# Moving operands of the first layer laid out as two runs, narrow blocks that alternate two feature chunks, and a new order

## The chip, the cores and the metric

One core of a Trainium2 chip runs the whole program. The time is the device time of one execution in microseconds (us); lower is better.

## What is computed

Attention with a block-causal mask, its heads laid side by side to 2304 tokens of 512 features, then two feed-forward layers.

```python
scores = scale * q @ k.T            # 4 batches, 8 heads, 576 tokens, 64 features a head
attn = softmax(where(block_i >= block_j, scores, -1e9))      # blocks of 64 tokens
x = (attn @ v) -> (2304, 512)
h = x @ w_in                        # 512 -> 2048
g = where(h >= 1, h, where(h <= -1, 0, (h + 1) ** 2 / 4))
x = g @ w_out                       # 2048 -> 512
h = x @ w2_in;  g = maximum(0.01 * h, h);  out = g @ w2_out  # second layer, the same sizes
```

## The kernel before, in words

Every product of the two layers is made of three matmuls in a 32-bit type that TensorE rounds (fp32r): both factors are split into a rounded part (hi) and the rest (lo), and hi*hi, hi*lo and lo*hi are summed in PSUM. A matmul holds one operand of 128x128 in the array (the stationary one, loaded anew for each matmul) and streams the other (the moving one) past it, column by column.

**Stage 1, attention with the first layer's h.** Attention is done in units of a head pair (lines L651 scores, L743 transposes, L762 and L770 values; scores and values use a quarter or a half of the array at a time). Between these, x @ w_in is done by blocks of tokens (`BLOCKS`): three narrow blocks of 256 tokens in `h1_block` (L877 for the first two pairs of feature chunks of block 0, L887 for all others) and three wide ones of 512 tokens in `h1_wide` (L855). The weights are stationary, x is the moving operand. In a narrow block two feature chunks j of 128 share one PSUM bank, 256 columns each; all 12 matmuls of chunk 0 run, then those of chunk 1, in pieces of four (kc = 0 to 3). A wide chunk fills a bank with 512 columns. `xbuf` gives x its places, `moe_load` fetches blocks 1 to 5 from DRAM (L813) and splits them (L815 on ScalarE, L816 on VectorE); block 0 is split where attention leaves it (`unit_values`). `w_float` makes the weights' halves (L508 to L523).

**Stage 2, the first layer's sums.** g @ w_out is done by a scheme with seven products in place of eight on half-size blocks (`ORDER`, `PRODUCTS`). The first 384 positions go through `y_group` (L1191), the other 768 through `y_unit` with `wide` true, three units of 256 positions. A unit takes eight steps p; each step loads four blocks of g, forms four differences (`t_forms`, L1211), splits both into hi and lo (L1236, L1237 on ScalarE, L1238, L1240 on VectorE), and does 7 products x 3 parts x 2 halves t = 42 matmuls of 256 columns (L1252). The weights are stationary; the moving operand, 256 positions of g, is one contiguous run, and serves both t.

**Stage 3, the second layer's h** (`h_step`, L1068, 288 columns), and **stage 4, the second layer's sums**: `y_unit` with `wide` false, the same 42 matmuls a step, but g is stationary and 256 columns of the weights move. `wc` hands these out as two runs of 128 columns that lie 384 or 512 elements apart:

```python
w = WC[m, p][c][g].get()[:, :, 128 * (i - 3 * g):128 * (i - 3 * g) + 128]
return w if e - a == 256 else w[:, a // 128]
```

Four units have 256 positions (t = 0, 1 take turns on each moving operand, each with its own half of the bank); the last has 128, so that each moving operand is used once and consecutive matmuls of a product add to the same 256 columns of PSUM.

**The order** of all instructions on all engines is made ahead by `Plan`: each step is an op with an engine, a modelled cost and a priority; `schedule` tries 400 list schedules from a random seed (`SEED`) and keeps the best. PE's ops are the groups that one `f` issues. All DMAs go through SP's queue.

Of the kernel before, what the change touches and what calls it, by code (L numbers as in the profile page):

```python
# [14 lines left out]
ALU = mybir.AluOpType  # L15
# [51 lines left out]

ENTRY = 105
SLACKS = (0, 800)
SEED, TRIES = 6, 400  # L70
LATEST, DRAWS = 0, 1


# [299 lines left out]
def fused_kernel(ctx, tc, qk, v, w1, w2, out):  # L373
# [92 lines left out]
    def xbuf(n, size):  # L466

        homes = (A0, A1)[n % 2], *LO[2 * (n % 2):2 * (n % 2) + 2]
        for home in homes:
            home.begin(F32R)  # L470
        hi, lo0, lo1 = (home.reg(0, m * size, shape=lambda ap, m=m: ap.rearrange("p (k t) -> p k t", k=m)) for home, m in zip(homes, (4, 2, 2)))
        return hi, (lo0, lo1)

    def xpart(x, c, kc):

        return (x[1][kc // 2], (kc % 2, kc % 2 + 1)) if c else (x[0], (kc, kc + 1))

    def xview(x, c, kc):
        buf, (k, _) = xpart(x, c, kc)
# [245 lines left out]
    def unit_values(pair, part, prio, ring, evac):  # L725
# [52 lines left out]
        if late is not None:  # L778
            dve(nq, prio, lambda: nc.vector.tensor_tensor(xp.get()[:, 0:nq], s.get()[:, 0, 0:nq], xp.get()[:, 0:nq], op=ALU.mult), [s, xp], [xp])
            if q0:  # L780
                x = XB[0]
                act(q0, prio, lambda: nc.scalar.activation(x[0].get()[:, kc], xp.get()[:, 0:q0], AF.Copy), [xp], [(x[0], (kc, kc + 1))], sb=True)
                dve(q0, prio, lambda: nc.vector.tensor_tensor(
                    xview(x, 1, kc), xp.get()[:, 0:q0], bc(x[0].get()[:, kc]), op=ALU.subtract), [xp, (x[0], (kc, kc + 1))],
                    [xpart(x, 1, kc)], port=True)
            dma(128 * (nq - q0) * 4, prio, lambda: nc.sync.dma_start(x1d[:, kc, c0 + q0:c0 + nq], xp.get()[:, q0:nq]), [xp],
                [(f"x1d{kc}", (c0 + q0, c0 + nq))])
            return
        if q0:
            x = XB[0]  # L790
            act(q0, prio, lambda: nc.scalar.activation(x[0].get()[:, kc], s.get()[:, 0, 0:q0], AF.Copy), [s], [(x[0], (kc, kc + 1))])
            dve(q0, prio, lambda: nc.vector.tensor_tensor(
                xview(x, 1, kc), s.get()[:, 0, 0:q0], bc(x[0].get()[:, kc]), op=ALU.subtract), [s, (x[0], (kc, kc + 1))], [xpart(x, 1, kc)])
        act(nq - q0, prio, lambda: nc.scalar.activation(xp.get()[:, 0:nq - q0], s.get()[:, 0, q0:nq], AF.Copy), [s], [xp])
        dma(128 * (nq - q0) * 4, prio, lambda: nc.sync.dma_start(x1d[:, kc, c0 + q0:c0 + nq], xp.get()[:, 0:nq - q0]), [xp],
            [(f"x1d{kc}", (c0 + q0, c0 + nq))])


    def moe_load(n, prio):
        i, m = BLOCKS[n]  # L800
        x = XB[n] = xbuf(n, 256 * m)
        if i == 0:
            return
        t0, tb = 256 * i, 256 * m
        for k in range(NKC):
            have = [q for _, q, wr in plan.regions.get(f"x1d{k}", []) if wr]
            assert all(any(q[0] <= z < q[1] for q in have) for z in range(t0, t0 + tb, 64)), (i, k)
        for j, lo in enumerate(x[1]):
            hi = (x[0], (2 * j, 2 * j + 2))

            def hv(j=j):
                return x[0].get()[:, 2 * j:2 * j + 2]
            dma(256 * tb * 4, prio, lambda lo=lo, j=j: nc.sync.dma_start(bc(lo.get()), x1d[:, 2 * j:2 * j + 2, t0:t0 + tb]),  # L813
                [(f"x1d{k}", (t0, t0 + tb)) for k in (2 * j, 2 * j + 1)], [lo])
            act(2 * tb, prio + X_SPLIT, lambda hv=hv, lo=lo: nc.scalar.activation(hv(), bc(lo.get()), AF.Copy), [lo], [hi], sb=True)  # L815
            dve(2 * tb, prio + X_SPLIT, lambda hv=hv, lo=lo: nc.vector.tensor_tensor(lo.get(), bc(lo.get()), bc(hv()), op=ALU.subtract),  # L816
                [lo, hi], [lo], port=True)

    def runs(pos0, n):
# [45 lines left out]
    def h1_block(n, p0, dp, hbanks):  # L865

        i, xt = BLOCKS[n][0], XB[n]
        for p in range(NP2):
            pr = p0 + 2 * dp * p
            ps = bank(hbanks[0])  # L870
            hbanks.append(hbanks.pop(0))
            early = i == 0 and p < EARLY
            for kc in range(NKC if early else 0):
                for j in range(2):
                    def f(fc=2 * p + j, j=j, kc=kc, ps=ps):
                        for k, (c, x) in enumerate(((0, 0), (1, 0), (0, 1))):
# [25 lines left out]
            h1_out(ps, parts, pr - 8)  # L902
# [294 lines left out]
    def t_forms(n, pv, raw, tt):  # L1197

        def g(i, k=1):
            return bc(raw.get()[:, n * i:n * (i + k)])  # L1200

        def t(i, k=1):
            return tt.get()[:, n * i:n * (i + k)]

        def two(ap):
            return ap.rearrange("p (s t) -> p s t", s=2)
        for cols, o, r, w, f in (
                (2 * n, 0, [raw], (0, 2), lambda: (two(t(0, 2)), g(3).unsqueeze(1).to_broadcast([128, 2, n]), two(g(1, 2)))),
                (n, 2, [raw, (tt, (0, 1))], (2, 3), lambda: (t(2), g(2), t(0))),
                (n, 3, [raw, (tt, (2, 3))], (3, 4), lambda: (t(3), g(0), t(2)))):  # L1210
            dve(cols, pv, lambda f=f: nc.vector.tensor_tensor(*f(), op=ALU.subtract), r, [(tt, w)], port=True)  # L1211
# [1 line left out]
    def y_unit(layer, pos0, n, p0, dp, banks_):  # L1213
# [11 lines left out]
        for p in range(NP2):  # L1225
# [3 lines left out]
            def s_(t, i, k=1):  # L1229
# [5 lines left out]
            t_forms(n, pv, raw, tt)  # L1235
            act(3 * n, pv, lambda raw=raw, hr=hr: nc.scalar.activation(s_(hr, 0, 3), bc(s_(raw, 0, 3)), AF.Copy), [(raw, (0, 3))], [hr], sb=True)  # L1236
            act(4 * n, pv, lambda tt=tt, ht=ht: nc.scalar.activation(s_(ht, 0, 4), s_(tt, 0, 4), AF.Copy), [tt], [ht], sb=True)  # L1237
            dve(3 * n, pv, lambda raw=raw, hr=hr: nc.vector.tensor_tensor(s_(raw, 0, 3), bc(s_(raw, 0, 3)), bc(s_(hr, 0, 3)), op=ALU.subtract),  # L1238
                [(raw, (0, 3)), hr], [(raw, (0, 3))], port=True)
            dve(4 * n, pv, lambda tt=tt, ht=ht, lt=lt: nc.vector.tensor_tensor(s_(lt, 0, 4), s_(tt, 0, 4), bc(s_(ht, 0, 4)), op=ALU.subtract),  # L1240
                [tt, ht], [lt], port=True)
            for o, m in enumerate(ORDER):
# [1 line left out]
                ps = P[m][0]  # L1244
                wh, zi = WHERE[ri]
                for k, (cw, x) in enumerate(((0, (hr, ht)[wh]), (1, (hr, ht)[wh]), (0, ((raw, (0, 3)), (lt, None))[wh]))):
                    def f(k=k, cw=cw, x=x[0] if isinstance(x, tuple) else x, ps=ps, li=li, zi=zi, p=p):
# [175 lines left out]
```

## Time and profile before

| | |
|---|---|
| three timed runs | 928.88, 934.44, 935.6 us (median 934.44) |
| the profiled execution | 928.28 us, of which the span of its instructions is 926.5 us |
| TensorE (PE) matmul busy | 915.6 us, 99% of the span |
| VectorE (DVE) / ScalarE (ACT) / GpSimd (POOL) busy | 727.7 / 519.6 / 293.9 us |

A matmul's record spans its passage through the array and overlaps with the next, so PE's busy share tells whether it was ever empty, not how fast it went. The pace is read from the chain of work that ended last: a piece such as "452.67 90.69 PE bank L1252 x770" is 770 matmuls that followed each other for 90.69 us.

### The profile page before, as it was taken

The page shows a single profiled execution, that of the slowest core. Times are in us where ns is not written, and L with a number is a line of the kernel's source. Part 1 is how long each engine was busy: PE and PEld are TensorE (multiplying, and loading weights), DVE is VectorE, ACT ScalarE, POOL GpSimd, SP SyncE. Part 2 cuts the span into 40 slices and gives each one's busy share as a digit, 9 for nine tenths or more (in the row PEclk, how much of TensorE's full clock was granted, in tenths as well). Part 3 has the DMA queues.
Part 4 walks back from the last instruction along what each step waited for, and adds up shares of the span by engine and source line. Part 5 has one row for each costly group of instructions (what it writes and reads, how often), then busy time and mean ns, then how long its engine had stood idle before and what let it go on. Part 6 is the DMA issues. An engine that isn't in the chain of part 4 may idle for free.

```text
span 926.5 us, 18684 instructions
## 1 busy us (share of the span) xinstructions
PE 915.6 (99%) x6818; PEld 827.7 (89%) x6818; DVE 727.7 (79%) x1247; ACT 519.6 (56%) x1014; POOL 293.9 (32%) x490
## 2 busy tenths in 40 slices
PE   9999999999999999999999999999999999999998
PEld 6687887876777878899999999999999999999998
DVE  6998677777777646559989798677879899888977
ACT  7788677787777666653434343344535664434333
POOL 5577787787665400000000040146445000000000
PEclk9999999999999999999999999999999999999999
DMA  8678788788799789656525499987887983544433
GB/s 310 212 224 249 236 281 285 261 275 272 273 315 323 276 263 325 191 172 209 154 84 161 140 348 337 346 290 269 266 279 242 328 269 91 176 132 139 148 91 115
DMA packets 164892, 216.72 MB, mean 234 GB/s; under 512 B 9920, under 2 KB 138432, under 8 KB 164800
## 3 DMA queue, kind: packets, MB, share of 16 engines
q1 hardware_dynamic: 164800, 215.52, 71.8%
q8 instruction: 54, 0.88, 0.4%
q14 instruction: 38, 0.31, 0.1%
HBM read 134.74 MB, written 80.74 MB: 233 GB/s over the span
## 4 chain that ended last, share of the span: by engine, by line
PE 92%; DVE 2%; DMA 2%; ACT 1%; issue 1%; POOL 1%; SPq 0%; POOLq 0%; DVEq 0%; ACTq 0%
PE bank L1252 31%; PE bank L1068 15%; PE bank L855 14%; PE bank L887 7%; PE bank L1191 6%; PE slot L651 5%; PE slot L770 5%; PE slot L743 5%; DMA rg<-gd 1%; DVE ra L976 1%; DMA wcd<-rg 1%; DMA rb<-x1d 1%; ACT rp L573 1%; PE bank L545 1%; PE slot L762 0%
## 5 line engine op out<-in xcount | busy, mean ns | idle before, releaser
L1068 PE MATMUL bank<-rp,w 128*128 128x288 f32 x1344 | 179.7, 294 | 1.2 <-ACT ra L978 0.9
L1068 PEld LDWEIGHTS bank<-rp,w 128*128 128x128 f32 x1344 | 178.1, 188 | 1.8 <-ACT ra L978 1.2
L976 DVE TENSOR_TENSOR ra<-ra,bank 128x288 f32<-128x288 f32 (+2 forms) x280 | 125.8, 488 | 43.7 <-ACT ra L978 21.8
L1252 PE MATMUL bank<-w,rp 128*128 128x256 f32 x1014 | 145.9, 277 | 0.0
L1252 PEld LDWEIGHTS bank<-w,rp 128*128 128x128 f32 x1014 | 129.8, 188 | 0.0
L855 PE MATMUL bank<-ra,w 128*128 128x512 f32 x384 | 100.0, 398 | 0.3 <-DVE rg L838 0.3
L1237 ACT ACTIVATE rp<-ra 128x1024 fp32r<-128x1024 f32 (+1 forms) x48 | 47.5, 991 | 72.5 <-DVE ra L1211 62.7
L855 PEld LDWEIGHTS bank<-ra,w 128*128 128x128 f32 x384 | 70.1, 188 | 17.1 <-issue 2.3
L838 DVE SCALAR_TENSOR_TENSOR rg<-bank,rg 128x512 f32<-128x512 f32 x72 | 49.3, 684 | 38.0 <-ACT rg L837 35.1
L1072 ACT ACTIVATE ra<-ra 128x1152 f32<-128x1152 f32 x32 | 37.3, 1167 | 71.4 <-DVE ra L976 71.4
L1252 PE MATMUL bank<-rp,w 128*128 128x256 f32 x508 | 76.6, 279 | 0.0
L936 POOL TENSOR_TENSOR w<-w 128x128 f32<-128x128 f32 x128 | 66.9, 543 | 26.7 <-DVE w L932 24.7
L1003 POOL TENSOR_TENSOR xs<-xs,rp 128x576 f32<-128x576 f32 x1 | 1.5, 1547 | 212.0 <-DMA xs<-x2d 212.0
L836 ACT ACTIVATE rg<-bank 128x512 f32<-128x512 f32 x72 | 43.1, 598 | 43.2 <-PE bank L855 36.6
L1252 PEld LDWEIGHTS bank<-rp,w 128*128 128x128 f32 x508 | 67.2, 188 | 0.0
L1240 DVE TENSOR_TENSOR rb<-ra,rp 128x1024 fp32r<-128x1024 f32 (+1 forms) x48 | 54.3, 1133 | 3.9 <-ACT rp L1237 0.7
L1252 PE MATMUL bank<-w,rb 128*128 128x256 f32 x294 | 57.0, 277 | 0.0
L887 PE MATMUL bank<-ra,w 128*128 128x256 f32 x352 | 53.6, 289 | 0.0
L855 PE MATMUL bank<-rb,w 128*128 128x512 f32 x192 | 53.1, 398 | 0.0
L887 PEld LDWEIGHTS bank<-ra,w 128*128 128x128 f32 x352 | 45.1, 188 | 3.5 <-issue 2.6
L1252 PE MATMUL bank<-rg,w 128*128 128x256 f32 x280 | 47.7, 279 | 0.0
L1236 ACT ACTIVATE rp<-rp 128x768 fp32r<-128x768 f32 (+1 forms) x33 | 26.4, 803 | 36.2 <-DMA rp<-gd 21.5
(169 smaller groups left out, 1977.6 us busy)
## 6 DMA issues: line engine op xcount, KB each, us to landing
rp<-gd SPq DMA_DIRECT2D x41, 512.0 KB, 4.2
wcd<-w SPq DMA_DIRECT2D x43, 448.0 KB, 4.6
gd<-ra SPq DMA_DIRECT2D x32, 576.0 KB, 4.8
gd<-rg SPq DMA_DIRECT2D x64, 256.0 KB, 3.6
w<-wcd SPq DMA_DIRECT2D x32, 512.0 KB, 5.7
w<-wcd SPq DMA_DIRECT2D x32, 384.0 KB, 5.7
w<-w SPq DMA_DIRECT2D x44, 256.0 KB, 4.6
w<-w SPq DMA_DIRECT2D x16, 512.0 KB, 5.1
```

The costliest lines, as they stand in the source:

```text
L651: nc.tensor.matmul(out, lhsT=x.get()[r, q:q + 128], rhs=x.get()[r, k0 + ka:k0 + kb], start=start, stop=True, skip_group_check=True)
L743: nc.tensor.transpose(s.get()[:, hd, o:o + 128], prob(hd, a, a + 128), ident.get())
L838: dve(512, pv, lambda: nc.vector.scalar_tensor_tensor(gt.get(), ps.get(), 1.0, gt.get(), op0=ALU.max, op1=ALU.min), [ps, gt], [gt])
L855: nc.tensor.matmul(ps.get(), lhsT=win(fc, c, kc), rhs=xview(xt, x, kc), start=(k == 0 and kc == 0), stop=(k == 2 and kc == NKC - 1), skip_ ...
L887: nc.tensor.matmul(ps.get()[:, 256 - j * 256:512 - j * 256], lhsT=win(fc, c, kc), rhs=xview(xt, x, kc), start=(k == 0 and kc == 0 and j == 0),
L936: plan.op("POOL", 430, prio, lambda o=o, a=a, b=b, op=op: nc.gpsimd.tensor_tensor(sl(o), sl(a), sl(b), op=op), [(fx, (a, a + 1)), (fx, (b, ...
L976: dve(cols, prio, lambda: nc.vector.tensor_tensor(out(o), out(a), P[b][1](), op=op), [P[b][0], (slots, (a, a + 1))], [(slots, (o, o + 1))])
L1068: nc.tensor.matmul(ps.get()[:, 0:HALF], lhsT=wc(1, p, cw, li, 128 * kc, 128 * kc + 128), rhs=r.get()[:, cx, kc], start=(k == 0 and kc == 0 ...
L1191: nc.tensor.matmul(ps[t].get()[:, 0:n], lhsT=wc(z, p, cw, li, 128 * t, 128 * t + 128), rhs=x.get()[:, n * zi:n * zi + n], start=(p == 0 an ...
L1237: act(4 * n, pv, lambda tt=tt, ht=ht: nc.scalar.activation(s_(ht, 0, 4), s_(tt, 0, 4), AF.Copy), [tt], [ht], sb=True)
L1240: dve(4 * n, pv, lambda tt=tt, ht=ht, lt=lt: nc.vector.tensor_tensor(s_(lt, 0, 4), s_(tt, 0, 4), bc(s_(ht, 0, 4)), op=ALU.subtract), [tt, ...
L1252: nc.tensor.matmul(ps.get()[:, 256 * t:256 * t + w], lhsT=b if wide else g, rhs=g if wide else b, start=(p == 0 and k == 0 and t == 0), st ...
```

## The change

Four things. (1) `xbuf` and the first layer's wide `y_unit` keep the moving operand as two runs: the first halves of all blocks, then the second halves (`h` is the outermost dimension). A moving operand of 256 columns is then two runs of 128, one of 512 columns two runs of 256. The lo part of g's own blocks (`one` in the code, 3 of the 21 product parts) stays one run. The engines that split and subtract write through views with one more dimension; `moe_load` needs two DMAs per half in place of one. (2) In `h1_block` the loops are turned: for each kc the two chunks j follow each other on the same moving operand; an op of PE is 8 matmuls, not 4, and needs the weights of both chunks. (3) `SEED` is 4, not 6. (4) With other ops and another seed, the whole order is new.

```diff
-SEED, TRIES = 6, 400
+SEED, TRIES = 4, 400
...
-        hi, lo0, lo1 = (home.reg(0, m * size, shape=lambda ap, m=m: ap.rearrange("p (k t) -> p k t", k=m)) for home, m in zip(homes, (4, 2, 2)))
+        hi, lo0, lo1 = (home.reg(0, m * size, shape=lambda ap, m=m: ap.rearrange("p (h k t) -> p k h t", h=2, k=m)) for home, m in zip(homes, (4, 2, 2)))
...
-            dma(256 * tb * 4, prio, lambda lo=lo, j=j: nc.sync.dma_start(bc(lo.get()), x1d[:, 2 * j:2 * j + 2, t0:t0 + tb]),
+            def load(lo=lo, j=j):
+                for k in range(2):
+                    nc.sync.dma_start(bc(lo.get())[:, k], two(x1d[:, 2 * j + k, t0:t0 + tb]))
+            dma(256 * tb * 4, prio, load,
...
-            for j in range(0 if early else 2):
-                fc = 2 * p + j
-                for k, (c, x) in enumerate(((0, 0), (1, 0), (0, 1))):
-                    def f(fc=fc, j=j, k=k, c=c, x=x, ps=ps):
-                        for kc in range(NKC):
-                            nc.tensor.matmul(ps.get()[:, 256 - j * 256:512 - j * 256], lhsT=win(fc, c, kc),
+            for k, (c, x) in enumerate(() if early else ((0, 0), (1, 0), (0, 1))):
+                def f(p=p, k=k, c=c, x=x, ps=ps):
+                    for kc in range(NKC):
+                        for j in range(2):
+                            nc.tensor.matmul(ps.get()[:, 256 - j * 256:512 - j * 256], lhsT=win(2 * p + j, c, kc),
...
-                    pe(4 * 118.2, pr + 0.01 * j, f, [(W[p], (2 * c + j, 2 * c + j + 1))] + [xpart(xt, x, kc) for kc in range(NKC)], [ps])
+                pe(8 * 118.2, pr + 0.01 * k, f, [(W[p], (2 * c, 2 * c + 2))] + [xpart(xt, x, kc) for kc in range(NKC)], [ps])
...
+    def forms(ap, n, k, runs_, split):
+
+        ap = ap[:, 0:k * n]
+        if runs_ == 1:
+            return ap.rearrange("p (i h t) -> p i h t", i=k, h=split)
+        return ap.rearrange("p (h i t) -> p i h t", i=k, h=runs_)
...
-                            g = x.get()[:, n * zi + a:n * zi + e]
+                            g = forms(x.get(), n, m, 2, 2)[:, zi] if wide and not one else x.get()[:, n * zi + a:n * zi + e]
```

The order of matmuls on PE in block 0 (L887 before, L898 after; `ra` and `rb` hold hi and lo of x, `w` the weights). Before, one pair of chunks:

```order
L887 MATMUL bank_90<-ra_1_307,w_1_638 128x256 x8
L887 MATMUL bank_90<-rb_1_322,w_1_638 128x256 x2
L887 MATMUL bank_90<-rb_1_480,w_1_638 128x256 x2
L887 MATMUL bank_90<-ra_1_307,w_1_638 128x256 x8
L887 MATMUL bank_90<-rb_1_322,w_1_638 128x256 x2
L887 MATMUL bank_90<-rb_1_480,w_1_638 128x256 x2
L743 MATMUL slot_129<-ident,rp_1_78 128x128 x8
```

After, the same pair:

```order
L898 MATMUL bank_90<-ra_1_317,w_1_664 128x256 x8
L654 MATMUL slot_152<-w_1_116 128x288
L654 MATMUL slot_129<-w_1_116 128x288
L654 MATMUL slot_152<-w_1_116 128x288
L654 MATMUL slot_129<-w_1_116 128x288
L898 MATMUL bank_90<-ra_1_317,w_1_664 128x256 x8
L898 MATMUL bank_90<-rb_1_323,w_1_664 128x256 x4
L898 MATMUL bank_90<-rb_1_485,w_1_664 128x256 x4
L746 MATMUL slot_130<-ident,rp_1_78 128x128 x8
```

The 24 matmuls of a pair come in three pieces of 8 and no longer in six of 4. Over the whole program, rows of full-array matmuls follow rows of attention's part-array ones (L651, L762, L770) 55 times before and 60 times after.

SP's queue at the start, where queries and keys (L635, L638 after), weights (L508, L511 after) and values (L644, L647 after) are fetched. Before:

```order
L635 DMA rp_1_95<-qk 128x2x320 x2
L508 DMA w_1_116<-w 128x1024
L508 DMA w_1_121<-w 128x1024
L635 DMA w_1_137<-qk 128x2x320
L644 DMA rp_1_95<-v 128x384
L508 DMA w_1_155<-w 128x1024
```

After:

```order
L638 DMA rp_1_95<-qk 128x2x320 x2
L638 DMA w_1_116<-qk 128x2x320
L647 DMA rp_1_95<-v 128x384
L511 DMA w_1_122<-w 128x1024
L647 DMA w_1_138<-v 128x384
L511 DMA w_1_146<-w 128x1024
L638 DMA rp_1_95<-qk 128x2x320
```

The first weight load now stands behind one more load of queries and keys and one of values. Later in the same queue the loads of x (L813, L824 after) of one narrow block read, before and then after:

```order
L925 DMA w_1_137<-w 128x2x256 x2
L813 DMA rb_1_881<-x1d 128x2x256
L635 DMA w_1_201<-qk 128x2x320
L644 DMA w_1_201<-v 128x384
L841 DMA gd_70<-rg_602 128x2x128
```

```order
L936 DMA w_1_116<-w 128x2x256 x2
L824 DMA rb_1_875<-x1d 128x2x128 x2
L853 DMA gd_70<-rg_608 128x2x128 x2
L638 DMA w_1_245<-qk 128x2x320
L647 DMA w_1_245<-v 128x384
```

One load has become two. There are 10 such rows before.

## Rows read from the trace of the kernel before

**Rows 1.** The page: span, busy time by engine, granted clock by slice.

```profile
span 926.5 us, 18684 instructions
PE 915.6 (99%) x6818; PEld 827.7 (89%) x6818; DVE 727.7 (79%) x1247; ACT 519.6 (56%) x1014; POOL 293.9 (32%) x490
PEclk9999999999999999999999999999999999999999
```

**Rows 2.** Windows by stage: busy us (instructions) by engine, granted clock, DMA share, GB/s.

```profile
0.00:50.00 50.00, 46.17 (x358) 34.20 (x358) 40.76 (x87) 38.50 (x119) 28.55 (x64) 1.00 0.78 256
50.00:202.00 152.00, 150.38 (x1235) 122.75 (x1235) 114.27 (x229) 116.13 (x333) 115.41 (x205) 1.00 0.82 260
202.00:330.00 128.00, 128.00 (x757) 92.83 (x757) 93.53 (x161) 94.49 (x222) 78.99 (x126) 1.00 0.84 285
453.50:543.50 90.00, 90.00 (x766) 90.00 (x766) 75.79 (x108) 37.16 (x43) 1.66 (x2) 1.00 0.53 166
```

**Rows 3.** The chain in order of time: start us, us, what.

```profile
126.69 1.89 PE bank L887 x16
...
380.09 15.59 PE bank L855 x68
...
452.67 90.69 PE bank L1252 x770
...
573.00 136.73 PE bank L1068 x1034
...
752.19 170.72 PE bank L1252 x1500
```

**Rows 4.** The chain in the window 913 to 923 us, the last unit of 128 positions.

```profile
912.88 10.02 PE bank L1252 x85
```

**Rows 5.** Groups of PE by line and form: x count, busy us, mean ns of one.

```profile
L855 PE MATMUL bank<-ra,w 128*128 128x512 f32 x384 | 100.0, 398 | 0.3 <-DVE rg L838 0.3
L887 PE MATMUL bank<-ra,w 128*128 128x256 f32 x352 | 53.6, 289 | 0.0
L855 PE MATMUL bank<-rb,w 128*128 128x512 f32 x192 | 53.1, 398 | 0.0
L887 PE MATMUL bank<-rb,w 128*128 128x256 f32 x176 | 28.8, 286 | 0.0
```

**Rows 6.** The chain: eight L887 matmuls behind attention's values, and eight within dense work.

```profile
48.86 1.14 PE bank L887 x8
...
99.49 0.95 PE bank L887 x8
```

**Rows 7.** The chain between 36 and 46 us.

```profile
36.51 0.98 DVE w L523
...
41.06 1.26 issue
...
42.36 1.60 POOL w L523
...
44.04 0.98 POOL w L510
```

**Rows 8.** Line L813, the loads of x: duration ns of the issue, min/median/max.

```profile
L813 SPq DMA_DIRECT2D rb<-x1d x10: 367/400/560, 65.5 to 335.0; - x10
```

**Rows 9.** The chain between 157 and 165 us.

```profile
157.29 6.42 DMA rb<-x1d
...
163.73 1.06 ACT ra L815
```

**Rows 10.** Groups of DVE by line and form (L750 reads two runs of 384).

```profile
L1211 DVE TENSOR_TENSOR ra<-rp,ra 128x256 f32<-128x256 f32 x82 | 34.1, 423 | 2.0
L750 DVE COPY rp<-slot 128x768 f32<-128x768 f32 x16 | 15.2, 949 | 5.2 <-PE slot L743 4.3 <-ACT rp L748 0.8
L1238 DVE TENSOR_TENSOR rp<-rp,rg 128x768 fp32r<-128x768 f32 x12 | 11.5, 957 | 1.0
L1211 DVE TENSOR_TENSOR ra<-rp,ra 128x128 f32<-128x128 f32 x12 | 3.5, 288 | 0.3
```

More of the change, by code (lines that the diff above doesn't have):

```diff
@@ L476, in xpart, with two @@
         return (x[1][kc // 2], (kc % 2, kc % 2 + 1)) if c else (x[0], (kc, kc + 1))
+    def two(ap):
+        return ap.rearrange("p (h t) -> p h t", h=2)
     def xview(x, c, kc):
@@ L781, in unit_values @@
                 x = XB[0]
-                act(q0, prio, lambda: nc.scalar.activation(x[0].get()[:, kc], xp.get()[:, 0:q0], AF.Copy), [xp], [(x[0], (kc, kc + 1))], sb=True)
+                act(q0, prio, lambda: nc.scalar.activation(x[0].get()[:, kc], two(xp.get()[:, 0:q0]), AF.Copy), [xp], [(x[0], (kc, kc + 1))], sb=True)
                 dve(q0, prio, lambda: nc.vector.tensor_tensor(
-                    xview(x, 1, kc), xp.get()[:, 0:q0], bc(x[0].get()[:, kc]), op=ALU.subtract), [xp, (x[0], (kc, kc + 1))],
+                    xview(x, 1, kc), two(xp.get()[:, 0:q0]), bc(x[0].get()[:, kc]), op=ALU.subtract), [xp, (x[0], (kc, kc + 1))],
                     [xpart(x, 1, kc)], port=True)
@@ L790, in unit_values @@
             x = XB[0]
-            act(q0, prio, lambda: nc.scalar.activation(x[0].get()[:, kc], s.get()[:, 0, 0:q0], AF.Copy), [s], [(x[0], (kc, kc + 1))])
+            act(q0, prio, lambda: nc.scalar.activation(x[0].get()[:, kc], two(s.get()[:, 0, 0:q0]), AF.Copy), [s], [(x[0], (kc, kc + 1))])
             dve(q0, prio, lambda: nc.vector.tensor_tensor(
-                xview(x, 1, kc), s.get()[:, 0, 0:q0], bc(x[0].get()[:, kc]), op=ALU.subtract), [s, (x[0], (kc, kc + 1))], [xpart(x, 1, kc)])
+                xview(x, 1, kc), two(s.get()[:, 0, 0:q0]), bc(x[0].get()[:, kc]), op=ALU.subtract), [s, (x[0], (kc, kc + 1))], [xpart(x, 1, kc)])
         act(nq - q0, prio, lambda: nc.scalar.activation(xp.get()[:, 0:nq - q0], s.get()[:, 0, q0:nq], AF.Copy), [s], [xp])
@@ L796, in unit_values, with halves @@
             [(f"x1d{kc}", (c0 + q0, c0 + nq))])
+    def halves(ap):
+        return ap.rearrange("p k h t -> p h k t")
     def moe_load(n, prio):
@@ L811, in hv, with lv @@
             def hv(j=j):
-                return x[0].get()[:, 2 * j:2 * j + 2]
-            dma(256 * tb * 4, prio, lambda lo=lo, j=j: nc.sync.dma_start(bc(lo.get()), x1d[:, 2 * j:2 * j + 2, t0:t0 + tb]),
+                return halves(x[0].get()[:, 2 * j:2 * j + 2])
+            def lv(lo=lo):
+                return halves(lo.get())
+            def load(lo=lo, j=j):
+                for k in range(2):
+                    nc.sync.dma_start(bc(lo.get())[:, k], two(x1d[:, 2 * j + k, t0:t0 + tb]))
+            dma(256 * tb * 4, prio, load,
                 [(f"x1d{k}", (t0, t0 + tb)) for k in (2 * j, 2 * j + 1)], [lo])
-            act(2 * tb, prio + X_SPLIT, lambda hv=hv, lo=lo: nc.scalar.activation(hv(), bc(lo.get()), AF.Copy), [lo], [hi], sb=True)
-            dve(2 * tb, prio + X_SPLIT, lambda hv=hv, lo=lo: nc.vector.tensor_tensor(lo.get(), bc(lo.get()), bc(hv()), op=ALU.subtract),
+            act(2 * tb, prio + X_SPLIT, lambda hv=hv, lv=lv: nc.scalar.activation(hv(), bc(lv()), AF.Copy), [lo], [hi], sb=True)
+            dve(2 * tb, prio + X_SPLIT, lambda hv=hv, lv=lv: nc.vector.tensor_tensor(lv(), bc(lv()), bc(hv()), op=ALU.subtract),
                 [lo, hi], [lo], port=True)
@@ L1195, in y_group, with t_forms @@
         y_sums(Y, grp, first, p0 + dp * NP2 - 12, P)
-    def t_forms(n, pv, raw, tt):
+    def forms(ap, n, k, runs_, split):
[3 more added lines that the diff above has]
+        return ap.rearrange("p (h i t) -> p i h t", i=k, h=runs_)
+    def t_forms(n, pv, raw, tt, runs_=1):
         def g(i, k=1):
-            return bc(raw.get()[:, n * i:n * (i + k)])
+            return forms(bc(raw.get()), n, 4, 1, runs_)[:, i:i + k]
         def t(i, k=1):
-            return tt.get()[:, n * i:n * (i + k)]
-        def two(ap):
-            return ap.rearrange("p (s t) -> p s t", s=2)
+            return forms(tt.get(), n, 4, runs_, runs_)[:, i:i + k]
         for cols, o, r, w, f in (
-                (2 * n, 0, [raw], (0, 2), lambda: (two(t(0, 2)), g(3).unsqueeze(1).to_broadcast([128, 2, n]), two(g(1, 2)))),
+                (2 * n, 0, [raw], (0, 2), lambda: (t(0, 2), g(3).to_broadcast([128, 2, runs_, n // runs_]), g(1, 2))),
                 (n, 2, [raw, (tt, (0, 1))], (2, 3), lambda: (t(2), g(2), t(0))),
@@ L1234, in y_unit @@
             pv = pr - 12
-            t_forms(n, pv, raw, tt)
-            act(3 * n, pv, lambda raw=raw, hr=hr: nc.scalar.activation(s_(hr, 0, 3), bc(s_(raw, 0, 3)), AF.Copy), [(raw, (0, 3))], [hr], sb=True)
+            r2 = 2 if wide else 1
+            t_forms(n, pv, raw, tt, r2)
+            act(3 * n, pv, lambda raw=raw, hr=hr, r2=r2: nc.scalar.activation(forms(hr.get(), n, 3, r2, r2), forms(bc(raw.get()), n, 3, 1, r2), AF.Copy), [(raw, (0, 3))], [hr], sb=True)
             act(4 * n, pv, lambda tt=tt, ht=ht: nc.scalar.activation(s_(ht, 0, 4), s_(tt, 0, 4), AF.Copy), [tt], [ht], sb=True)
-            dve(3 * n, pv, lambda raw=raw, hr=hr: nc.vector.tensor_tensor(s_(raw, 0, 3), bc(s_(raw, 0, 3)), bc(s_(hr, 0, 3)), op=ALU.subtract),
+            dve(3 * n, pv, lambda raw=raw, hr=hr, r2=r2: nc.vector.tensor_tensor(forms(raw.get(), n, 3, 1, r2), forms(bc(raw.get()), n, 3, 1, r2), forms(bc(hr.get()), n, 3, r2, r2), op=ALU.subtract),
                 [(raw, (0, 3)), hr], [(raw, (0, 3))], port=True)
@@ L1246, in y_unit, with f @@
                 for k, (cw, x) in enumerate(((0, (hr, ht)[wh]), (1, (hr, ht)[wh]), (0, ((raw, (0, 3)), (lt, None))[wh]))):
-                    def f(k=k, cw=cw, x=x[0] if isinstance(x, tuple) else x, ps=ps, li=li, zi=zi, p=p):
+                    def f(k=k, cw=cw, x=x[0] if isinstance(x, tuple) else x, ps=ps, li=li, zi=zi, p=p, m=4 - (wh == 0), one=k == 2 and wh == 0):
                         for t in range(nt):
```

## The prediction

> **What bounds the kernel now.** I read the page first, for which engine is never empty: PE is busy for 915.6 of 926.5 us, every slice reads 9, and the granted clock is 1.00 throughout, the higher of its two levels, 2.4 GHz [rows 1]. The stage windows say the same of the places that the change touches: 150.38 of 152 us beside attention with the narrow blocks, 128 of 128 with the wide ones, 90 of 90 in the sums [rows 2]. Only the first 50 us have holes (46.17). So after the start the time is a number of matmuls times a pace, and the question is the pace.
>
> The chain of waits gives it, as pieces of matmuls without a gap [rows 3]. At 2.4 GHz, 256 columns alone would take 106.7 ns, 288 columns 120.0, 512 columns 213.3. Measured start to start:
> - first layer's sums, one run of 256: 90.69 us / 770 = 117.8 ns
> - narrow blocks, one run of 256: 1.89 us / 16 = 118.1 ns
> - wide blocks, one run of 512: 15.59 us / 68 = 229.3 ns
> - second layer's h, one run of 288: 136.73 us / 1034 = 132.2 ns
> - second layer's sums, two runs of 128, last unit: 10.02 us / 85 = 117.9 ns [rows 4]
> - second layer's sums, two runs of 128, the four full units: the piece of 1500 ends with the last unit's 8 x 21 = 168 matmuls, so (170.72 - 168 x 0.1179) / 1332 = 113.3 ns.
>
> The first and the last line are the point: the same 42 matmuls of 256 columns a step, the same clock, the same alternation of two halves of a bank, and a pace that differs by 4.5 ns. What differs is that the moving operand is one run in the first layer and two runs in the second. The last unit has two runs as well and still goes at the slow pace; it differs from the full units in that each moving operand serves one matmul, not two, and consecutive matmuls add to the same columns of PSUM. So the trace has the gain only where two runs come together with turn-taking, and it does not tell which half of the turn-taking matters.
>
> **The change, part by part.**
>
> *The sums (L1252, first layer).* 3 units x 8 steps x 42 = 1008 matmuls; 18 of 21 parts become two runs, 864 matmuls, which is the second layer's full unit in every respect that I named. 864 x 4.5 ns = -3.9 us, all of it on the path, since PE is never empty there. Bounds: 0 to 1008 x 4.5 = 4.5 us.
>
> *The narrow blocks (L887).* 352 + 176 = 528 matmuls [rows 5]. Two runs plus two chunks that take turns on the operand and on the halves of a bank: the same two conditions. 528 x 4.5 ns = -2.4 us. PE is busy for 150.38 of 152 us there, so nearly all should reach the end; attention's chain could keep some, so 0 to 2.4. Block 0's first two pairs (L877) keep their order and stand among the waits of the first 50 us: 0.
>
> *The wide blocks (L855).* 384 + 192 = 576 matmuls [rows 5] get two runs of 256 but no turns: each moving operand serves one matmul, and the next adds to the same 512 columns. The nearest row is the last unit, 117.9 ns [rows 4], which is the slow pace. I take 0. At the other end the surcharge of a long run shrinks in proportion to the columns, 2 x 4.5 = 9.0 ns a matmul, 576 x 9.0 = -5.2 us.
>
> *Coarser pieces and the new order.* PE goes from attention's part-array rows to full-array ones 60 times, not 55. Eight matmuls behind attention's values take 1.14 us, eight within dense work 0.95 [rows 6], so an entry costs at most 0.19 us: 5 x 0.19 = +1.0 us. An op of 8 needs the weights of both chunks; where block 0 runs, PE's chain passes through the making of weights (0.98 us L523, 1.60 us L523, 0.98 us L510, between 36 and 46 us [rows 7]), and the first weight load now stands behind two more loads on SP's queue, 320 + 192 KB, which at the 256 GB/s of this stretch [rows 2] is 2.0 us. Against that, queries, keys and values come earlier by about as much. I take 0, with 2.0 us to either side.
>
> *Ten more DMA issues.* A load of x is now two, each issue 0.40 us [rows 8]: 10 x 0.40 = 4.0 us of SP's queue. SP holds up what is queued behind, loads of attention's units and stores of g, which are issued well ahead. One load of x is on the chain, at 157.29 us, with ScalarE's split waiting behind it [rows 9]; there the second half comes one issue later. I take +0.4, between 0 and 4.0. The pieces that a DMA moves are half as long; the landing of 6.42 us in that row could grow, which is within that bound.
>
> *VectorE and ScalarE.* The columns are the same, the views have more runs. VectorE reading 768 columns in two runs takes 949 ns, in one run 957 [rows 10]: a run costs nothing that shows. 0, with the other end under the rivals.
>
> **The sum** is -3.9 - 2.4 + 1.0 + 0.4 = -4.9 us. Against the profiled execution that is 928.28 - 4.9 = 923.4. The four executions shown lie in two groups, 928.28 and 928.88, 934.44 and 935.6, with nothing in the trace of the faster one that tells why. Their mean is 931.8, and the median of the timed three is in the upper group; 934.44 - 4.9 = 929.5. I take the mean: 931.8 - 4.9 = 926.9, so 927.
>
> **The rivals.**
>
> *The wide blocks gain too.* If the last unit is slow for a reason of its own and two runs alone are what counts, the wide blocks give up to 5.2 us more: 926.9 - 5.2 = 921.7. For it: the surcharge over the bare columns is 11.1 ns at 256 and 16.0 at 512, so it does grow with the length of a run. Against it: rows 4.
>
> *The layout does nothing in the first layer.* The 4.5 ns may belong to what moves (weights that stand still for the whole stage, against g that has just been written) and not to the runs. Then the 6.3 us fall away and the costs remain: 931.8 + 1.4 = 933.2. For it: in the rows, runs and kind of operand change together. Against it: the last unit moves the same weights, and is slow. The Trainium skill (TensorE: Matmul & The Clock Gate, Back-to-back issue gap) speaks for this rival: it gives the warm gap as the columns divided by 2.4 GHz plus about 2.5 ns, with no term for how the operand lies; by that rule both layouts would take 109.2 ns. The trace disagrees with the figure in either layout and shows two paces for the same columns, so I give the rule little weight.
>
> *VectorE becomes the bound of the sums, and the kernel is slower.* Per step VectorE is busy for 75.79 / 90 [rows 2] of 42 x 117.8 ns = 4.95 us, that is 4.17 us. A step's four operations on g and its differences grow from 5 runs to 14 on their widest side. If each of the 9 further runs cost what a new instruction costs (288 ns for 128 columns, 423 for 256, so 135 ns per 128 and 153 ns fixed [rows 10]), a step would need 4.17 + 1.38 = 5.55 us, and 24 steps would take 24 x 0.60 = 14.4 us longer than now: 931.8 + 14.4 - 2.4 + 1.4 = 945.2. It decides from about 91 ns a run, where the step exceeds today's 4.95 us by enough to eat the rest. Against it: 949 against 957 ns [rows 10].
>
> **How the numbers follow.** The sum as it stands 0.50; the wide blocks too 0.18; no effect of the layout 0.20; VectorE's bound 0.04; the rest, 0.08, is the new start order, 2.0 us to either side. The likeliest gives 927. The range 917 to 936 reaches from the lower group with the wide blocks (928.28 - 4.9 - 5.2 = 918.2) and a start that comes out well, to the upper group with nothing gained. One per cent, 9.3 us, is about what a measurement of this kernel can tell from no change, its own runs being 6.7 us apart. Faster by more than that means under 925.1 against the median: 0.27 of the first case, which needs the lower group, most of the second, a little of the others, together 0.34. Slower by more than that is VectorE's case and a bad start, 0.05. Within it 0.61.
>
> **What would show it.** In the changed profile the chain's piece of the first layer's sums (line L1269) should go at (36 x 113.3 + 6 x 117.8) / 42 = 113.9 ns; the narrow blocks (L898) at about 113 within dense work, eight of them in 0.91 us; the wide ones (L867) at 229. VectorE's 768-column subtraction should stay near 957 ns, and second layer's h and sums at 132 and 113. A piece of L867 at 220 to 225 would mean the first rival, L1269 at 118 the second, a wait of PE on VectorE between sums the third. Wrong altogether would be a hole on PE in the first 100 us that outweighs the 5 us, from the weights of two chunks arriving late.

## The result and the profile after

The changed kernel takes 934.4 us (median of 12 runs, 931.13 to 936.72), the kernel before beside it 928.68 us (12 runs, 927.53 to 935.6). The ratio is 1.0053, with a 95% interval of 1.0036 to 1.007: half a per cent slower, where 5 us faster had been forecast. Nine of the 12 runs of before lie between 927.5 and 928.9 us and three between 933.3 and 935.6; the median of 934.44 us that was known ahead of the change came from such a handful. The profiled execution took 934.2 us, with a span of 932.4 us.

The page of the changed kernel, beside [rows 1]:

```profile
span 932.4 us, 18684 instructions
PE 922.1 (99%) x6818; PEld 833.3 (89%) x6818; DVE 730.7 (78%) x1247; ACT 518.1 (56%) x1014; POOL 290.6 (31%) x490
PEclk9999999999999999999999999999999999999999
```

As many matmuls as before, TensorE again hardly ever empty after the start, the same granted clock. So the 5.9 us are a pace. The chain of the changed kernel, in order of time (start us, us, what), beside [rows 3]; L898 is the old L887, L867 the old L855, L1269 the old L1252, L1079 the old L1068:

```profile
127.96 1.89 PE bank L898 x16
...
353.81 13.75 PE bank L867 x60
...
452.93 90.72 PE bank L1269 x770
...
572.72 135.01 PE bank L1079 x1021
...
752.43 176.44 PE bank L1269 x1498
```

- Narrow blocks with two runs and turn-taking: 1.89 / 16 = 118.1 ns, to the digit what it was.
- Wide blocks: 13.75 / 60 = 229.2 ns, as before.
- First layer's sums with two runs: 90.72 / 770 = 117.8 ns, as before.
- Second layer's h: 135.01 / 1021 = 132.2 ns, as before.
- Second layer's sums, whose code, operands and loops the change does not touch: 176.44 / 1498 = 117.8 ns, where the full units went at 113.3.

The starts of the pieces say where the time arose. The first layer's sums begin at 452.93 us (452.67 before), the second layer's at 752.43 (752.19). Everything that the change does up to there, the layout, the turns, the entries, the DMAs, the new order, adds up to +0.24 us. From there to the end it is 932.4 - 752.43 = 179.97 us against 926.5 - 752.19 = 174.31: +5.7 us in the one stage that the change leaves alone.

The stage windows (busy us and instructions of PE, PEld, DVE, ACT, POOL; granted clock; DMA share; GB/s) of the changed kernel, beside [rows 2]:

```profile
0.00:50.00 50.00, 44.77 (x350) 33.07 (x351) 39.41 (x83) 37.30 (x117) 26.67 (x63) 1.00 0.74 245
50.00:202.00 152.00, 151.89 (x1234) 123.10 (x1233) 115.83 (x231) 115.83 (x332) 117.81 (x210) 1.00 0.84 266
453.50:543.50 90.00, 90.00 (x767) 90.00 (x766) 74.59 (x112) 36.42 (x41) 0.55 (x1) 1.00 0.54 165
755.00:895.00 140.00, 140.00 (x1191) 140.00 (x1190) 119.61 (x170) 57.83 (x63) 0.00 (x0) 1.00 0.45 137
```

And the last of these windows in the kernel before:

```profile
755.00:895.00 140.00, 140.00 (x1238) 140.00 (x1237) 123.43 (x180) 60.80 (x67) 0.00 (x0) 1.00 0.46 140
```

The new order has 1.4 us more holes in the first 50 us and 1.5 fewer up to 202, which cancels. In 755 to 895 us both kernels have TensorE full at a granted clock of 1.00, and the changed one gets 47 matmuls fewer through. Nobody waits: the same instruction simply takes another step. The view of one line's instructions (duration in ns, least/median/most) shows it matmul by matmul. Before, 760 to 890 us:

```profile
L1252 PE MATMUL bank<-w,rp x784: 275/276/277, 760.0 to 890.0; 128*128 128x256 f32 x196
```

After, the same stretch:

```profile
L1269 PE MATMUL bank<-w,rp x750: 281/281/281, 759.8 to 889.9; 128*128 128x256 f32 x188
```

A record's duration is thus a mark of the pace: 275 to 277 ns with 113.3 from start to start, 278 to 281 with 117.8. I call them the **short** and the **long pace**.

### The profile page after: what moved, and what is told of

Same layout as the page of the kernel before. It is cut to its first block, busy times and chain, and to the rows that moved or that the text cites. A ratio compares the mean times of both kernels' runs of the same rounds, so it can differ in the third digit from the quotient of the medians.

```text
span 932.4 us, 18684 instructions
## 1 busy us (share of the span) xinstructions
PE 922.1 (99%) x6818; PEld 833.3 (89%) x6818; DVE 730.7 (78%) x1247; ACT 518.1 (56%) x1014; POOL 290.6 (31%) x490
## 4 chain that ended last, share of the span: by engine, by line
PE 91%; DVE 4%; issue 2%; ACT 2%; DMA 2%; POOL 0%; DVEq 0%; ACTq 0%; POOLq 0%; SPq 0%
PE bank L1269 32%; PE bank L1079 15%; PE bank L867 14%; PE bank L898 7%; PE bank L1202 6%; PE slot L746 5%; PE slot L773 5%; PE slot L654 5%; DVE ra L987 1%; DMA rp<-qk 1%; DMA gd<-ra 1%; ACT rp L576 1%; DVE w L975 1%; PE bank L548 0%; DVE nmb L569 0%
## 5 line engine op out<-in xcount | busy, mean ns | idle before, releaser
L1079 PE MATMUL bank<-rp,w 128*128 128x288 f32 x1344 | 179.8, 294 | 0.6 <-DVE ra L987 0.6
L1079 PEld LDWEIGHTS bank<-rp,w 128*128 128x128 f32 x1344 | 178.2, 188 | 1.2 <-DVE ra L987 0.8
L1269 PE MATMUL bank<-w,rp 128*128 128x256 f32 x1014 | 149.8, 281 | 0.0
L1269 PEld LDWEIGHTS bank<-w,rp 128*128 128x128 f32 x1014 | 133.1, 189 | 0.0
L867 PE MATMUL bank<-ra,w 128*128 128x512 f32 x384 | 100.0, 399 | 0.8 <-DVE rg L850 0.7
L867 PEld LDWEIGHTS bank<-ra,w 128*128 128x128 f32 x384 | 69.6, 188 | 18.0 <-DVE rg L850 2.4
L1269 PE MATMUL bank<-rp,w 128*128 128x256 f32 x508 | 73.9, 279 | 0.0
L947 POOL TENSOR_TENSOR w<-w 128x128 f32<-128x128 f32 x128 | 61.5, 503 | 15.1 <-DVE w L943 13.7
L1269 PEld LDWEIGHTS bank<-rp,w 128*128 128x128 f32 x508 | 66.0, 188 | 0.0
L1269 PE MATMUL bank<-w,rb 128*128 128x256 f32 x294 | 57.9, 281 | 0.0
L867 PE MATMUL bank<-rb,w 128*128 128x512 f32 x192 | 52.8, 398 | 0.0
L898 PE MATMUL bank<-ra,w 128*128 128x256 f32 x352 | 51.1, 289 | 0.0
L898 PEld LDWEIGHTS bank<-ra,w 128*128 128x128 f32 x352 | 44.0, 188 | 5.3 <-issue 4.4
L1227 DVE TENSOR_TENSOR ra<-rp 128x512 f32<-128x512 f32 (+2 forms) x51 | 35.6, 699 | 15.8 <-DMA rp<-gd 15.1
```

What stands on the lines that cost most here:

```text
L867: nc.tensor.matmul(ps.get(), lhsT=win(fc, c, kc), rhs=xview(xt, x, kc), start=(k == 0 and kc == 0), stop=(k == 2 and kc == NKC - 1), skip_ ...
L947: plan.op("POOL", 430, prio, lambda o=o, a=a, b=b, op=op: nc.gpsimd.tensor_tensor(sl(o), sl(a), sl(b), op=op), [(fx, (a, a + 1)), (fx, (b, ...
L1079: nc.tensor.matmul(ps.get()[:, 0:HALF], lhsT=wc(1, p, cw, li, 128 * kc, 128 * kc + 128), rhs=r.get()[:, cx, kc], start=(k == 0 and kc == 0 ...
```

## The experiments

**Two paces** (theory 1 from here on): 256 columns have two paces that hold themselves; which one a gapless stretch gets is settled where it begins, and neither the layout nor the loops set it. **The layout:** the prediction's theory, that two runs with turn-taking make the short pace, and something else slows the second layer. **The order:** what runs beside the matmuls in the new order sets their pace. Each expectation says what the theories that it weighs would give.

### The layout alone, with the old order: e1_layout

The two-run layouts of the change in `xbuf`, `moe_load` and `y_unit` (`forms`), the old loops of `h1_block`, and

```diff
-SEED, TRIES = 4, 400
+SEED, TRIES = 6, 400
```

so that TensorE and VectorE run in the order of before.

> The kernel before with the two-run layout alone: the order on every engine is that of before, only the loads of x are two in place of one. Theory 1 (two paces): 256-column matmuls with a new weight load each go at one of two steady paces, 113.3 or 117.8 ns; which one a gapless stretch takes is decided as it is entered, not by how the moving operand lies. Then the first layer's sums stay at 117.8 ns, the narrow blocks at 118, the second layer's sums enter as before and go at 113.3 in most executions: 928 to 930 us. Theory 2 (layout): something in the first layer's two-run layout slows the second layer's sums; they go at 117.8, 934 us. Theory 3 (what I predicted): first layer's sums at 113.9, 924 us.

Measured: 928.19 us, ratio 1.0002 (0.9981 to 1.0023). The chain:

```profile
452.61 90.69 PE bank L1270 x770
...
752.49 158.95 PE bank L1270 x1402
```

The first layer's sums have two runs, turn-taking, everything that was said to make the short pace, and take 90.69 us for 770, exactly as with one run [rows 3]. The theory of the layout falls: it neither gives nor costs anything that shows, and nor do its ten further DMA issues. The second layer's 158.95 / 1402 = 113.4 ns reaches to 911.4 us, into the last unit, whose matmuls take no turns (905 to 916 us of this kernel):

```profile
L1270 PE MATMUL bank<-w,rp x65: 275/276/293, 905.1 to 915.8; 128*128 128x256 f32 x65
```

### The new order and loops alone, with one run: e2_order

The reverse: the changed kernel without its layout.

```diff
-                            g = forms(x.get(), n, m, 2, 2)[:, zi] if wide and not one else x.get()[:, n * zi + a:n * zi + e]
+                            g = x.get()[:, n * zi + a:n * zi + e]
```

> The changed kernel with all moving operands of the first layer as one run: the order on every engine is that of the changed kernel. Theory 1: as the changed kernel, second layer's sums at 117.8 ns in nearly all executions, 934 us; first layer's sums at 117.8. Theory 2: the second layer's sums are back at 113.3, 928 us.

Measured: 934.75 us, ratio 1.0054 (1.0036 to 1.0073), the loss of the whole change. The second layer's sums are long throughout (176.44 us for 1498). But the first layer's sums, with one-run operands, have this (chain in the window 461 to 532 us):

```profile
460.90 71.17 PE bank L1251 x628
```

71.17 / 628 = 113.3 ns: the short pace with one run, in a stage that never had it in before or after. Three microseconds later, in the same stage, with the same code, it is gone (durations in 461 to 531 and 535 to 541 us):

```profile
L1251 PE MATMUL bank<-rp,w x372: 276/276/276, 460.7 to 530.9; 128*128 128x256 f32 x186
...
L1251 PE MATMUL bank<-rp,w x15: 279/279/280, 534.8 to 540.9; 128*128 128x256 f32 x15
```

So no property of the operand sets the pace.

### Another order of the kernel before: e8_seed

```diff
-SEED, TRIES = 6, 400
+SEED, TRIES = 4, 400
```

> The kernel before with seed 4 in place of 6, nothing else: another order, old layout, old loops. Theory 1: the time is that of before or of the changed kernel by the pace that the second layer's sums (and perhaps a stretch of the first layer's) happen to take, 928 to 935 us, and the profile's pieces account for the difference. If the order itself matters by its waits in the first 330 us, holes of PE differ by several us.

Measured: 935.52 us, ratio 1.0068 (1.0052 to 1.0084), four runs. With the old layout and the old loops, a new order is enough to lose the short pace in the second layer's sums:

```profile
753.53 177.39 PE bank L1252 x1506
```

177.39 / 1506 = 117.8 ns. This could still be the order as such. The next kernels keep the order and disturb TensorE on purpose.

### A small disturbance, many times: e3_kick (in after) and e4_kickb (in before)

In each of the 40 steps of the second layer's sums one matmul of 256 columns is cut into two of 128; the computation is the same.

```diff
+                            if not wide and k == 1 and li == 0 and t == 0:
+                                for y in range(2):
+                                    nc.tensor.matmul(ps.get()[:, 256 * t + 128 * y:256 * t + 128 * y + 128], lhsT=g, rhs=b[:, y],
...
+                                continue
```

> The changed kernel, and in the second layer's sums one matmul of 256 columns of each step (40 in all) is issued as two of 128 columns; the result is the same, the order too. Each split costs about 100 ns if nothing else happens: 934.4 + 40 x 0.1 = 938.4 us. Theory 1: each split disturbs the stream, and behind some of them it goes on at 113.3 until the next one; pieces of both paces, each uniform between two splits, in one execution. With half of the pieces fast, 938.4 - 3.0 = 935.4. Theory 2, or an order of products that is itself slow: 117.8 throughout, 938.4.

> The kernel before with the same 40 splits. Theory 1: pieces of both paces as in the run on the changed kernel; 928.7 + 4 to 928.7 + 10 us by the share of slow pieces. If the fast pace belongs to the order of before and not to how the stretch is entered, the stream is back at 113.3 behind every split: 932.7 us.

Measured: e3_kick 933.53 us (ratio 1.0031, 1.001 to 1.0052), e4_kickb 932.83 us (ratio 1.0036, 1.0021 to 1.0051). In e3_kick (L1271 are the halves) the stretch that follows the first two cuts and the last matmuls of 288 columns is still long; from the third cut on the stretches are short:

```profile
752.30 0.17 PE bank L1271 x2
...
753.41 8.48 PE bank L1274 x72
761.89 0.17 PE bank L1271 x2
762.06 6.52 PE bank L1274 x57
...
839.56 8.80 PE bank L1274 x77
```

8.48 / 72 = 117.8 ns, and 6.52 / 57 = 114.4 and 8.80 / 77 = 114.3 with the restart behind the cut (one step of 170 to 173 ns). The durations of the same kernel, 754 to 760 and 840 to 848 us:

```profile
L1274 PE MATMUL bank<-w,rp x33: 281/281/281, 753.8 to 760.0; 128*128 128x256 f32 x33
...
L1274 PE MATMUL bank<-w,rp x46: 276/276/279, 839.8 to 847.8; 128*128 128x256 f32 x46
```

The order around these matmuls is that of after, in which 1498 of them went at 117.8 ns. The theory of the order falls with it: a disturbance of TensorE alone moves the pace. In e4_kickb the short pace survived the cuts, except at the end (long from 924.6 us on); one of its stretches:

```profile
843.18 7.21 PE bank L1257 x63
```

7.21 / 63 = 114.4 ns with the restart. The 40 cuts cost e4_kickb 932.83 - 928.62 = 4.2 us, beside before in the same batch, 0.11 us each. That is why neither kernel wins.

### Few cuts: e5_unit8 (in before) and e9_fix (in after)

One cut in each of the eight units of both layers' sums (e5_unit8), and four in the first unit of the second layer's (e9_fix).

```diff
+                            if p == 1 and k == 1 and li == 0 and t == 0:
```

```diff
+                            if not wide and pos0 == 0 and p in (1, 2, 3, 4) and k == 1 and li == 0 and t == 0:
```

> The kernel before, with one 256-column matmul issued as two of 128 in the second step of each of the eight units of the sums (three of the first layer, five of the second). Theory 1, with what the 40 splits showed (38 of 40 stretches behind a split went at 113): the first layer's sums go at 113 from the first split on, 90 of 118 us or more, -3.4 to -4.3 us; the second layer's stay at 113 in all executions, so none near 934; 8 splits cost 8 x 0.12 = 1.0 us: about 925.5. If the first layer's sums cannot go at 113 with one run and stationary weights, 929.6.

> The changed kernel with four splits of one 256-column matmul into two of 128, in steps 1 to 4 of the first unit of the second layer's sums; order and layout are the changed kernel's. Theory 1: out of the slow pace a split was followed by the fast one 2 of 6 times so far (into the fast pace it always led back), so with four tries the stream is fast from one of them on in about 4 of 5 executions; then the whole loss of the change is gone: 934.4 - 5.5 + 4 x 0.12 = 929.4 us. If the order or the layout of the changed kernel keeps these sums slow, 934.4 + 0.5 = 934.9.

Measured, e5_unit8: 928.87 us, ratio 0.9996 (0.9981 to 1.001). In the first layer's sums a cut left the pace long and the next one made it short:

```profile
458.06 39.27 PE bank L1258 x333
...
497.50 38.03 PE bank L1258 x335
```

117.9 and 113.5 ns, in one stage of one kernel in the order of before. The third unit's cut left the pace long again, so that one unit of three was won; the 925.5 us hoped for was missed. Measured, e9_fix: 933.69 us, ratio 1.0041 (1.0016 to 1.0066), but the seven runs are of two kinds: 928.99, 929.78, 929.9 and 933.69 to 934.36. The profiled one took 929.78. Its chain is short before the second cut: the first cut and the last matmuls of 288 columns are followed by the short pace:

```profile
752.11 0.17 PE bank L1271 x2
...
753.22 8.19 PE bank L1274 x72
...
770.89 153.47 PE bank L1274 x1345
```

8.19 / 72 = 113.8 and 153.47 / 1345 = 114.1 ns; the three later cuts kept it. Three of seven runs came in under 930 us, of the changed kernel without cuts none of 12 (lowest 931.13). So the cuts bring the pace back in some executions and not in others: it is not decided by the program alone.

### Is it only 256 columns? e6_h, e7_wide and e10_sweep (in before)

Cuts of 288 columns into two of 144 in the second layer's h (32 times), of 512 and 384 columns in halves in the wide blocks and `y_group` (48 and 16 times), and unequal cuts (32 to 224 columns) in the first layer's sums (24 times).

```diff
+                        if k == 1 and li == 0 and kc == 0:
...
+                                nc.tensor.matmul(ps.get()[:, 144 * y:144 * y + 144], lhsT=wc(1, p, cw, li, 128 * kc, 128 * kc + 128),
```

```diff
+                        if k == 1 and kc == 1:
...
+                                nc.tensor.matmul(ps.get()[:, 256 * y:256 * y + 256], lhsT=win(fc, c, kc), rhs=xview(xt, x, kc)[:, 256 * y:256 * y + 256],
```

```diff
+                                s = (32, 64, 96, 160, 192, 224)[(pos0 // 256 * 8 + p) % 6]
+                                for y, e in ((0, s), (s, 256)):
```

> The kernel before, with one 288-column matmul of each step of the second layer's h issued as two of 144 (32 splits). If two paces exist at 288 columns as well, the stretches behind the splits go at 120.0 + 6.7 = 126.7 ns and not at 132.2: 1344 x 5.5 = -7.4 us against 32 x 0.12 = +3.8, 925.0. If 288 columns have one pace, 928.6 + 3.8 = 932.4.

> The kernel before, with one 512-column matmul of each wide chunk (48) issued as two of 256, and one of each step of the first 384 positions (16) as two of 192. If two paces exist there too, 512 columns go at 220 ns and not 229, 384 columns at 166.7 and not 173.3: up to 576 x 9 = -5.2 and 336 x 6.6 = -2.2 us against 64 x 0.12 = +7.7: 929 to 930. If not, 936.

> The kernel before with a split in each of the 24 steps of the first layer's sums, unequal ones in turn: 32, 64, 96, 160, 192, 224 columns and the rest. Theory 1: some splits end a slow stretch, some a fast one, and each stretch between two is uniform at 113 or 118; the run shows which split does which. If the first layer's sums are fast for most of 118 us: 928.6 - 4 + 24 x 0.12 = 927.5; if none helps, 931.5.

Measured: e6_h 930.79 us (ratio 1.0029, 1.0014 to 1.0043), e7_wide 932.28 us (ratio 1.0042, 1.0026 to 1.0058), e10_sweep 933.48 us (ratio 1.0053, 1.0025 to 1.0081). In e6_h all stretches behind cuts kept one pace, in e7_wide as well. A stretch of each, of e6_h:

```profile
621.76 6.52 PE bank L1073 x49
```

of e7_wide (wide blocks, then `y_group`):

```profile
386.91 2.52 PE bank L860 x11
...
438.89 5.41 PE bank L1201 x31
```

6.52 / 49 = 133.1 ns, 2.52 / 11 = 229.1 and 5.41 / 31 = 174.5, the restart behind the cut included; undisturbed it is 132.2 and 229.3 [rows 3], and 50.27 / 289 = 173.9 for 384 columns in the chain of after:

```profile
399.89 50.27 PE bank L1202 x289
```

So cuts show no second pace at these widths. But 512 columns have one: in before, with no cut, 24 matmuls of a wide block that stand between matmuls of 384 columns (chain in 373 to 381 us):

```profile
373.10 1.04 PE bank L1191 x6
374.14 5.60 PE bank L855 x24
```

5.60 / 24 = 233.3 ns, where the piece at 380.09 us [rows 3] goes at 229.3; the same 24 take 5.60 us in e1_layout and in e6_h. So the two paces are not a matter of 256 columns alone. At 288 and 384 one was seen.

The unequal cuts: the first (96 + 160) was followed by the short pace, and behind the third (192 + 64) and all later ones it was long. Chain of e10_sweep:

```profile
452.95 4.91 PE bank L1258 x43
...
463.95 7.75 PE bank L1258 x65
...
483.25 9.37 PE bank L1258 x79
```

114.2, 119.2 and 118.6 ns with their restarts. In this execution unequal cuts were no remedy. The eight runs of e10_sweep lie in two groups, 930.18 to 931.46 and 935.5 to 937.67 us, and the median of 933.48 stands for neither.

### The pace held short in both kernels: e11_guard (before) and e12_guarda (after)

Twenty equal cuts: four in the first unit's steps 1, 2, 3 and 5 (in the first layer, the unit that begins at position 384), two in each other unit.

```diff
+                            if k == 1 and li == 0 and t == 0 and (p in (1, 2, 3, 5) if pos0 == (384 if wide else 0) else p in (1, 5)):
```

> The kernel before with 20 equal splits: steps 1, 2, 3 and 5 of the first unit of either layer's sums, steps 1 and 5 of the other units. Theory 1: both layers' sums are fast for most of their length in most executions; first layer -3 us if it is fast for three quarters of 118 us, splits 20 x 0.12 = +2.4, second layer as before but without the executions near 934: 928 us, spread 926.5 to 930.

> The changed kernel with the same 20 splits. Theory 1: each split out of the slow pace ends it in about 4 of 10 cases, and the fast pace survives splits, so the second layer's sums are fast from some step of the first two units on in nearly all executions, and the first layer's in most: 928 us, spread 926.5 to 932. If the changed order or layout holds its sums at the slow pace, 934.4 + 2.4 = 936.8.

Measured: e11_guard 927.74 us (926.9 to 930.21, 12 runs), ratio 0.9989 (0.9975 to 1.0003); e12_guarda 927.89 us (926.82 to 929.95, 12 runs), ratio 0.9976 (0.9955 to 0.9997). The changed kernel with 20 cuts is 934.4 - 927.9 = 6.5 us faster than without. Its second layer's sums:

```profile
771.15 22.72 PE bank L1275 x199
...
848.51 20.36 PE bank L1275 x179
```

114.2 and 113.7 ns. The first layer's sums have it too (view of one line, 464 to 531 us), 276 ns where after and before had the long pace:

```profile
L1275 PE MATMUL bank<-rp,w x337: 276/276/332, 463.8 to 530.8; 128*128 128x256 f32 x169
```

With the pace alike the medians of the two kernels are 0.15 us apart, which 12 runs each that spread over 3 us cannot tell from nothing: the change itself is worth nothing that shows. The gain over before is small, since 20 cuts take back 20 x 0.11 = 2.2 us of the 672 x 4.5 ns = 3.0 us that the first layer gives (672 of its 1008 matmuls follow the one before at the short pace in e11_guard's trace).

## Why the prediction was wrong

**The step that failed** is the reading of two rows as the effect of a layout: "the same 42 matmuls of 256 columns a step, the same clock, the same alternation of two halves of a bank, and a pace that differs by 4.5 ns. What differs is that the moving operand is one run in the first layer and two runs in the second." The 4.5 ns are right; they belong to neither layout nor loops. e1_layout gives the first layer two runs and gets 117.8 ns; e2_order leaves it one run and gets 113.3 over 628 matmuls. In the place of that reading the runs showed two paces of the same matmul, and a stretch keeps the one with which it began. With the new order the second layer's sums, which the prediction left at 113, began at the long one: +5.7 us. That 934.4 us lies within the forecast 917 to 936 is no support: the range reached so far for nothing gained in the upper group, not for a stage made slower.

**The last unit** was its support, "the slow pace" for want of turn-taking. It was the pace lost at one moment. The chain in two windows of before, 896 to 904.6 us and 905 to 912.8:

```profile
895.92 8.73 PE bank L1252 x77
...
904.99 7.90 PE bank L1252 x67
```

113.4 and 117.9 ns, with the change of pace between, behind a single step of 123 ns at 904.82 us. In e1_layout steps of 127 and 122 ns stand at the same matmul (905.1 us), and the unit runs on at 276 ns, as above.

**The trace of before had the counter-example,** and I did not look for it: narrow blocks, one run, no turns, at the short pace. Line L887 in 82.3 to 83.6 and in 126.9 to 128.5 us:

```profile
L887 PE MATMUL bank<-ra,w x8: 276/276/384, 82.1 to 83.0; 128*128 128x256 f32 x8
...
L887 PE MATMUL bank<-ra,w x8: 279/280/280, 127.0 to 127.8; 128*128 128x256 f32 x8
```

From start to start these are 113.3 and 117.7 ns. I compared one piece of each stage by its mean. The spread within a stage would have told that the two paces occur under one layout.

**The sums, -3.9 us, and the narrow blocks, -2.4 us:** measured 0 and 0 (117.8 and 118.1 ns, before and after).

**The wide blocks, 0:** right at 229.2 ns, but by luck: the reason given, the last unit that is slow for want of turns, does not hold.

**Entries +1.0, DMA issues +0.4, the start 0:** together +0.24 us up to 752.43 us. The 20 loads of x are issued as forecast (359/451/1297 ns), and nothing waited for them:

```profile
L824 SPq DMA_DIRECT2D rb<-x1d x20: 359/451/1297, 65.3 to 333.1; - x20
```

**VectorE and ScalarE, 0:** right. The subtraction of 768 columns through two-run views takes what it took [rows 10], here in the first layer's sums alone (452 to 573 us, ns least/median/most):

```profile
L1255 DVE TENSOR_TENSOR rp<-rp,rp x11: 950/958/961, 457.6 to 518.1; 128x768 fp32r<-128x768 f32 x11
```

**The two groups of runs.** The prediction met 928.3 and 928.9 beside 934.4 and 935.6 "with nothing in the trace of the faster one that tells why", and took their mean as its base. Their distance is that of the two paces in the second layer's full units: 1344 x 4.5 ns = 6.0 us. Of before, 16 of 110 runs took over 933 us; of e5_unit8, e11_guard and e12_guarda, which restart the pace again and again, none of 35 took over 930.3. No execution of before in the upper group was profiled, so that its second layer ran long is inferred from this and from e9_fix's two kinds of runs, not seen. What the change did is to move nearly every run into the group that before falls into now and then.

**The rivals.** "The layout does nothing in the first layer" came true in its mechanism; its time, 933.2, missed that the second layer loses. On the profiled executions: 928.28 + 0.24 + 5.7 = 934.2, as measured. The Trainium skill's rule that was cited for it (TensorE: Matmul & The Clock Gate, Back-to-back issue gap) has no term for the layout, and in that the runs agree. The Trainium skill gives that rule for a single matmul, not for a stream in which each has its weight load, as here; its 109.2 ns for 256 columns was seen in no stretch. VectorE's bound did not show.

**What stays open:** what in TensorE holds either pace, and which entry leads to which. Seen were only that equal cuts nearly always keep the short pace, that they end the long one some of the time, and that it also changes at places without a cut. One thing narrows it. In the traces of all 14 kernels the sums never change pace within an even stretch: each change stands at a step of 122 ns or more, or next to matmuls of another width. Such a step is where the pace can change, but not every one changes it: at the same matmul the changed kernel has a step of 149 ns (458.66 us) and goes on long, e2_order one of 153 ns (460.24 us) and goes on short.

## What to carry to other kernels

Where one operation has two paces, look at the spread within each stage before a difference between stages is put down to what the code does differently there; one counter-example in the trace ends such a theory for nothing. Two groups of runs a fixed distance apart can be a term to be found (here a count times a difference of pace) and not noise to be averaged. When a change makes a stage slower that it does not touch, exchange the order alone and the data alone before the change is blamed.

## What the hardware showed that was not expected

- fp32r matmuls of 256 columns, each with its own weight load, go at 113.3 or 117.8 ns from start to start, both at a granted clock of 1.00, and hold either for over 1300 matmuls in a row (the long one for 1506 in e8_seed). 512 columns go at 229.3 ns, and in one place at 233.3. 288 and 384 columns showed one pace each (132.2, 173.9 ns), cut or not.
- Cutting one matmul of 256 columns into two of 128 costs about 0.11 us, one of 288 into two of 144 about (930.79 - 928.49) / 32 = 0.07.
- A moving operand in two runs costs TensorE, and views in two runs cost VectorE, nothing that shows.
